# Reordering the set-up of a windowed-attention and feed-forward kernel on one Trainium2 core

## The chip, the core and the metric

The kernel runs on one core of one Trainium2 chip. A core has a matrix engine (TensorE, PE in the profile), a vector engine (VectorE, DVE), a scalar engine (ScalarE, ACT), a general engine (GpSimd, POOL) and a synchronising engine (SyncE, SP). Each runs its own list of instructions in order; they wait for one another and for transfers by semaphores. Transfers (DMA) are issued from POOL or SP in this kernel: the profile calls POOL's queue q0 and SP's q1. The metric is the device time of one execution in microseconds (us).

## The reference

There are 8 batches of 8 heads, 576 positions and head size 64, in float32. Position pairs count if they are at most 32 apart, or if one of the two is among 8 "global" positions given by index. A feed-forward layer with a sine follows.

```python
mask = np.abs(pos[:, None] - pos[None, :]) <= 32
mask = mask | is_global[:, None] | is_global[None, :]
scores = np.where(mask, scale * (q @ k.T), -1e9)
x = softmax(scores) @ v                     # then heads side by side: 4608 x 512
h = x @ w_in                                # 512 -> 2048
s = np.sin(alpha * h)
out = (h + s * s / (alpha + 1e-9)) @ w_out  # 2048 -> 512
```

## The kernel before

The order of the instructions is the order in which the program writes them down; no scheduler moves them. Work goes by batch. `attention(b)` computes the scores of a batch for four pairs of heads: 12 blocks of keys for a pair, in three groups of four (`scores`, a PSUM tile called `ring`). ACT takes the exponential (tile `E`), DVE multiplies by the 0/1 tile `MASK`, PE multiplies by V and sums (`products`, tiles `zn`, `zd`), ACT makes the reciprocal by Ln and Exp, and DVE writes the normalised result (`xT`, or `xlast` for odd batches). `gemm1(b)` is the first matrix product with the sine, in 16 steps (`nt`) of 128 columns. `gemm2(b)` is the second, and its matmuls are dealt out one by one between those of the next batch (`fill`).

For each batch the keys lie in a tile `KX`, the queries in `QX` and the values in `VX`, in two copies by parity of the batch. In each 64-wide block of `KX` and `VX` the last part holds the 8 global rows, so these have to be written there too. `KX` and `QX` of batch 0 come from natural loads (`nat`, in the tile `H2`, shown as `H`), which PE transposes (`turn_part`) and ACT and DVE copy into place (`place_part`). From batch 1 on, the keys and queries are cast in DRAM (`cast_qk`), transposed by DMA from SP's queue (`turn_qk`), and copied into place by DVE (`place`).

Three things concern the global rows. For batch 0, three indirect gathers by the row numbers in `grow` bring them as `g0k`, `g0q` and `VG0`; PE transposes the first two (tile `pg`) and ACT spreads them (`place_global_keys`, `place_global_queries`). For later batches, SP gathers the global rows of all batches (`gather` into `gk`, `gq`, `gv`), PE and DVE turn the first two into `kTg` and `qTg` (`turn_kq`), and POOL spreads them (`place_globals`). POOL casts `gv` to `VGb` (`cast_globals_v`), and `load_vg` copies rows of it into `VX` by SP's queue.

`MASK` is made in the set-up: six iotas on POOL (`qrel`, `qpos`, `jrow`), squares on ACT, and comparisons on DVE (`band`, and then a correction called `far`, for which the index lists `gp64` and `gidx8` have to be in). V, the four column blocks of `w_in` and the four row blocks of `w_out` are loaded from POOL's queue, each with a cast. A one-element copy `seen` on POOL waits for the transposed keys of batch 1; what POOL issues after it is held until then.

Of the kernel before, what the change touches and what calls it, by code (L numbers as in the profile page):

```python
# [10 lines left out]
ALU = mybir.AluOpType  # L11
AF = mybir.ActivationFunctionType
DT = mybir.dt
# [3 lines left out]
P = 128  # L17
KW = 96
NG = 8
KT = 48  # L20
WCOL = 120
# [4 lines left out]
PAD = 16  # L26
# [221 lines left out]
def kernel(  # L248
# [11 lines left out]
    nc = tc.nc  # L260
    B, H, S, D = q.shape
    DM, DFF = moe_w_in.shape
    WIN = 32
# [102 lines left out]
    def place_globals(b):  # L366

        for hp in range(NHP):
            for t in range(2):
                rows = slice(t * D, (t + 1) * D)  # L370
                nc.gpsimd.tensor_copy(
                    out=KX[b % 2][rows, hp, :, t * D + KT : t * D + KT + NG],
                    in_=kTg[rows, hp, None, :, b].to_broadcast([D, NT12, NG]),
                )
        for y in range(2):
            nc.gpsimd.tensor_copy(
                out=globals_of(b, slice(0, P), y),
                in_=qTg[:, :, None, y::2, b].to_broadcast([P, NHP, 7, 4]),
            )
# [67 lines left out]
    make_identity(nc, identb[:])  # L447
    qrel = setup.tile([P, 2, 2, WCOL // 2], DT.float32, name="qrel")
    for par, left in ((0, PAD), (1, 40)):
        nc.gpsimd.iota(qrel[:, par, :, 0:left], pattern=[[1, 2], [2, left]], base=-WIN,  # L450
                       channel_multiplier=0, allow_small_or_imprecise_dtypes=True)
        nc.gpsimd.iota(qrel[:, par, :, left:60], pattern=[[1, 2], [2, 60 - left]],
                       base=2 * left - 40, channel_multiplier=0, allow_small_or_imprecise_dtypes=True)
    qpos = setup.tile([P, NT12, 2, 24], DT.float32, name="qpos")
    nc.gpsimd.iota(qpos[:], pattern=[[KT, NT12], [1, 2], [2, 24]], base=0, channel_multiplier=0,
                   allow_small_or_imprecise_dtypes=True)
    jrow = setup.tile([P, NG], DT.float32, name="jrow")
    nc.gpsimd.iota(jrow[:], pattern=[[1, NG]], base=0, channel_multiplier=0,
                   allow_small_or_imprecise_dtypes=True)


    g64 = setup.tile([NG * B, 1], DT.int64, name="g64")
# [69 lines left out]
    )  # L532
    nc.vector.tensor_copy(out=grow[:], in_=rowf[0 : NG * B, 4:5])
    nc.vector.memset(kflat[:, half : 2 * half], 0.0)
    nc.vector.memset(tiny[:], TINY)
# [13 lines left out]

    g0 = {}  # L550
    for name, src in (("k", k), ("q", q), ("v", v)):
        g0[name] = VG0 if name == "v" else setup.tile([NG * B, D], DT.bfloat16, name="g0" + name)
        nc.gpsimd.indirect_dma_start(
            out=g0[name][:], out_offset=None, in_=src[0].rearrange("h s d -> (h s) d"),
            in_offset=bass.IndirectOffsetOnAxis(ap=grow[:, 0:1], axis=0),
        )
# [71 lines left out]
    def place_global_queries(t, copy):  # L628
        for y in range(2):
# [5 lines left out]
            )  # L635

    gpf = setup.tile([P, 1], DT.float32, name="gpf")
    nc.vector.tensor_copy(out=gpf[:], in_=gp64[:].bitcast(DT.int32)[:, 0:1])
    nc.scalar.activation(out=qpos[:], in_=qpos[:], func=AF.Square, bias=gpf[:, 0:1], scale=-1.0)
    gf = setup.tile([P, NG], DT.float32, name="gf")  # L640
    nc.vector.tensor_copy(out=gf[:], in_=gidx8[:].bitcast(DT.int32)[:, 0::2])
# [3 lines left out]
    )  # L645
    later = setup.tile([P, NG], DT.float32, name="later")
    nc.vector.tensor_scalar(
        out=later[:], in0=jrow[:], scalar1=pm, scalar2=float(-KT), op0=ALU.subtract, op1=ALU.is_ge
    )
# [3 lines left out]
    nc.vector.scalar_tensor_tensor(  # L653
        out=cond[:, 2:3], in0=pm, scalar=float(KT + NG - 1), in1=cond[:, 1:2], op0=ALU.is_le, op1=ALU.mult
    )
# [12 lines left out]
    turn_part(1, 0, views([zn[:, n, :] for n in range(2)]))  # L668
    for n in range(2):
        place_part(1, 0, n, act)  # L670
    turn_part(0, 0, views([zd[:, n, :] for n in range(2)]))
    for n in range(2):
        place_part(0, 0, n, dve)
    for w, name in ((1, "k"), (0, "q")):
        pg[w] = both[0:D, 32 + w * 64 : 64 + w * 64].bitcast(DT.bfloat16)
        nc.tensor.transpose(
            out=pg[w][:], in_=g0[name][:], identity=identb[0 : NG * B, 0 : NG * B]
        )
    nc.tensor.transpose(out=both[:, 0:NT], in_=arow[:], identity=idf[0:NT, 0:NT])
    for t in range(2):  # L680
        place_global_keys(t, act)
        place_global_queries(t, act)
    act(out=alphaT[:], in_=both[:, 0:NT])
    turn_part(0, 1, views([z[:] for z in zo]))
# [282 lines left out]
    def gemm1(b):  # L967
# [28 lines left out]
        for nt in range(NT):  # L996
# [217 lines left out]
```

## Time and profile before

| | us |
|---|---|
| median of three runs (lowest, highest) | 368.57 (367.44, 368.85) |
| the profiled execution | 368.04 |
| its span, first to last instruction | 366.3 |
| PE busy in the span | 337.0 (92%) |
| DVE, ACT, POOL busy | 283.8, 293.2, 138.2 |
| first key transpose on PE | 6.87 |
| first scores on PE | 16.14 |
| first step of `gemm1(0)` on PE | 33.30 |
| first scores of batch 1 on PE | 54.23 |

The span is shorter than the time of the execution by 1.74 us. A line of a timeline gives the start, the duration, the engine, the line of the program, the operation, what it writes and reads, and how many instructions were merged; in square brackets stands how long the engine sat idle before it, and what it waited for. A row of a DMA queue gives packets, megabytes and the time of the packets as a share of 16 DMA engines. The granted TensorE clock is 0.998 in this execution.

### The profile page before, as it was taken

To read this page: it belongs to the slowest core of one execution; us is meant where nothing else is said; L and a number is where in the kernel's file an instruction comes from. 1 tells how busy PE (TensorE), PEld (TensorE's weight loads), DVE (VectorE), ACT (ScalarE), POOL (GpSimd) and SP (SyncE) were. 2 spreads that over 40 slices of the span, in tenths; PEclk is the share of its full clock that TensorE was granted. 3 is DMA by queue.
4 is the path that set the end of the run, shared out by engine and by line. 5 is a ranking of instruction groups with operands and counts; after the bars stand their busy time and mean duration, and the time that the engine had idled before them with its cause. 6 is when DMAs were issued, how large, how long until landed. Compare 5 with 4: busy or idle time off the path is not lost.

```text
span 366.3 us, 8428 instructions
## 1 busy us (share of the span) xinstructions
PE 337.0 (92%) x3040; PEld 227.8 (62%) x3040; DVE 283.8 (77%) x621; ACT 293.2 (80%) x566; POOL 138.2 (38%) x246
## 2 busy tenths in 40 slices
PE   2578968999999899999999999999999999999993
PEld 2467655766567666767667756776676766655441
DVE  6776998598878877888887887888788866789560
ACT  7689997887888688887889887979888888879510
POOL 7983696568864532660076205720000000000001
PEclk9999999999999999999999999999999999999999
DMA  6999999999999794989198904638111001000311
GB/s 124 112 156 186 175 148 190 150 146 200 161 201 221 78 107 106 174 94 149 30 167 111 146 30 54 82 30 158 45 46 30 0 30 60 29 3 20 96 57 53
DMA packets 103579, 38.07 MB, mean 104 GB/s; under 512 B 94138, under 2 KB 98250, under 8 KB 103082
## 3 DMA queue, kind: packets, MB, share of 16 engines
q0 software_dynamic: 56640, 18.56, 44.1%
q1 hardware_dynamic: 46890, 18.89, 26.2%
q8 instruction: 26, 0.43, 0.5%
q14 instruction: 23, 0.19, 0.2%
HBM read 37.15 MB, written 17.83 MB: 150 GB/s over the span
## 4 chain that ended last, share of the span: by engine, by line
PE 66%; DVE 9%; ACT 5%; issue 2%; DMA 1%; POOL 0%; POOLq 0%; DVEq 0%; ACTq 0%
PE zo L1047 29%; PE zn L990 9%; PE zr L990 8%; PE zd L990 7%; PE zd L783 4%; PE ring L741 4%; PE zn L783 4%; DVE H L1028 3%; ACT sb L1020 2%; DVE QX L349 2%; DVE s L1026 1%; PE zr L783 1%; ACT osb L1053 1%; DVE xT L815 1%; ACT s L1024 1%
## 5 line engine op out<-in xcount | busy, mean ns | idle before, releaser
L1047 PE MATMUL zo<-w_out,H 128*128 128x512 bf16 x576 | 153.7, 379 | 0.0
L990 PEld LDWEIGHTS <-w_in 128*128 128x128 bf16 x1024 | 98.6, 98 | 47.1 <-issue 10.8
L393 POOL DMA_DIRECT2D VX<-in_v_dram x128 | 82.7, 657 | 90.8 <-PE zd L783 63.1
L1047 PEld LDWEIGHTS <-H 128*128 128x128 bf16 x576 | 52.3, 97 | 37.2
L749 ACT ACTIVATE E<-ring 128x480 bf16<-128x480 f32 x96 | 54.2, 567 | 23.0 <-PE ring L741 22.7
L752 DVE TENSOR_TENSOR E<-E,MASK 128x480 bf16<-128x480 bf16 x96 | 35.9, 405 | 17.5 <-ACT E L749 16.2
L1075 POOL DMA_INDIRECT out_dram<-osb,grow x1 | 1.0, 998 | 121.0 <-SPq L1182 121.0
L1028 DVE SCALAR_TENSOR_TENSOR H<-s,recipT,zn 128x576 bf16<-128x576 bf16 x47 | 38.2, 813 | 10.3 <-ACT s L1024 6.6
L1024 ACT ACTIVATE s<-sb 128x576 bf16<-128x576 bf16 (+1 forms) x62 | 42.7, 689 | 2.0
L741 PE MATMUL ring<-QX,KX 128*128 128x120 bf16 x384 | 37.2, 221 | 7.3 <-ACT E L749 3.2
L1020 ACT ACTIVATE sb<-zn,alphaT 128x576 bf16<-128x576 f32 (+1 forms) x47 | 34.8, 739 | 11.2 <-PE zn L990 11.2
L741 PEld LDWEIGHTS <-KX 128*128 128x128 bf16 x384 | 28.3, 100 | 23.0 <-issue 10.8
L1028 DVE SCALAR_TENSOR_TENSOR H<-s,recipT,zd 128x576 bf16<-128x576 bf16 x39 | 31.7, 814 | 6.5 <-ACT s L1024 4.6
L1028 DVE SCALAR_TENSOR_TENSOR H<-s,recipT,zr 128x576 bf16<-128x576 bf16 x39 | 31.7, 813 | 4.2 <-ACT s L1024 2.1
L1020 ACT ACTIVATE sb<-zd,alphaT 128x576 bf16<-128x576 f32 (+1 forms) x39 | 28.9, 740 | 7.1 <-PE zd L990 7.0
L1026 DVE TENSOR_TENSOR s<-sb 128x576 bf16<-128x576 bf16 (+1 forms) x66 | 30.6, 463 | 4.1 <-ACT sb L1020 3.8
L1020 ACT ACTIVATE sb<-zr,alphaT 128x576 bf16<-128x576 f32 (+1 forms) x39 | 28.9, 740 | 5.6 <-PE zr L990 5.6
L783 PEld LDWEIGHTS <-VX 128*128 128x128 bf16 x448 | 25.9, 98 | 9.3 <-issue 3.3
L990 PE MATMUL zn<-xT,w_in 128*128 128x288 bf16 x184 | 26.9, 286 | 3.5 <-DVE H L1028 2.0
L1053 ACT COPY osb<-zo 128x512 f32<-128x512 f32 x36 | 20.8, 577 | 11.3 <-PE zo L1047 10.0
L990 PE MATMUL zn<-xlast,w_in 128*128 128x288 bf16 (+1 forms) x192 | 28.8, 289 | 0.4
L783 PE MATMUL zn<-E,VX 128*128 128x120 bf16 (+2 forms) x336 | 26.3, 209 | 1.0 <-DMA VX<-VGb 0.6
(159 smaller groups left out, 489.9 us busy)
## 6 DMA issues: line engine op xcount, KB each, us to landing
VX<-in_v_dram POOLq DMA_DIRECT2D x128, 36.0 KB, 5.8
kd<-in_k_dram POOLq DMA_DIRECT2D x7, 576.0 KB, 7.3
qd<-in_q_dram POOLq DMA_DIRECT2D x7, 576.0 KB, 9.5
w_in<-in_moe_w_in_dram POOLq DMA_DIRECT2D x4, 512.0 KB, 5.7
w_out<-in_moe_w_out_dram POOLq DMA_DIRECT2D x4, 512.0 KB, 8.7
out_dram<-osb SPq DMA_DIRECT2D x8, 256.0 KB
out_dram<-osb SPq DMA_DIRECT2D x8, 224.0 KB
out_dram<-osb SPq DMA_DIRECT2D x8, 192.0 KB
```

Of the source, the lines that this page charges most:

```text
L393: nc.gpsimd.dma_start(out=VX[b % 2][r : r + 24, hp, :, t * D : t * D + D], in_=v[b, 2 * hp + t].rearrange("(i a y) d -> y a i d", a=24, y= ...
L741: nc.tensor.matmul(out=ps[:, e * WCOL : (e + 1) * WCOL], lhsT=kx[:, hp, i, :], rhs=qx[:, hp, :, s0 : s0 + 60], start=True, stop=True, skip ...
L749: nc.scalar.activation(out=Eg, in_=ps[:, 0 : 4 * WCOL], func=AF.Exp, scale=scale, accum_out=EA[:, n : n + 1])
L752: nc.vector.tensor_tensor(out=Eg, in0=Eg, in1=MASK[:, 4 * g : 4 * g + 4, :].rearrange("p i c -> p (i c)"), op=ALU.mult,)
L783: nc.tensor.matmul(out=out_t[:, half, :, a - half * CUT : z - half * CUT], lhsT=OB[:] if key else VXb[:, hp, i, :], rhs=E[:, i, :, a - s0 ...
L990: nc.tensor.matmul(out=h[e][:, 0:W], lhsT=lhsT, rhs=xT[:, c, e, 0:W], start=(c == 0), stop=(c == CT - 1), skip_group_check=True,)
L1020: nc.scalar.activation(out=sb[:, es, 0:W], in_=h[:, :, 0:W], func=AF.Sin, scale=alphaT[:, nt : nt + 1])
L1024: nc.scalar.activation(out=s2[:, :, 0:W], in_=sb[:, :, 0:W], func=AF.Square)
L1026: nc.vector.tensor_tensor(out=s2[:, :, 0:W], in0=sb[:, :, 0:W], in1=sb[:, :, 0:W], op=ALU.mult)
L1028: nc.vector.scalar_tensor_tensor(out=H2[:, nt, r0 : r0 + S].rearrange("p (e c) -> p e c", e=2)[:, es], in0=s2[:, es, 0:HALF], scalar=recip ...
L1047: nc.tensor.matmul(out=ops[:], lhsT=H2[:, nt, blk * P : (blk + 1) * P], rhs=w_out[:, nt, :], start=(nt == 0), stop=(nt == NT - 1),)
L1053: nc.scalar.copy(out=osb[:], in_=ops[:])
```

## The change

Instructions of the set-up and of the end of batch 0 are put in another order, and one group of copies is merged. The amount of computation is the same.

- On POOL the gathers of `g0k` and `g0q` stand right behind the computation of `grow`, and the six iotas behind them. The first block of `w_in` is issued next, then the gather of V's global rows, then V of pairs 0, 1 and 2.
- ACT clears the second half of `VX[0]` before it squares `qrel`.
- The key and query copies of batch 0 stand before the correction of `MASK`, which comes after the global columns. Two short comparisons and `gpf` stay ahead of the query copies.
- Block 2 of `w_in` is issued right behind the casts of batch 1, block 3 right behind POOL's memsets and before SP turns the keys and `seen` is written. Before, both came after `seen`. V of pair 1 of batch 1 moves from there to step 11 of `gemm1(0)`.
- At step 11 of `gemm1(0)`, the order on POOL was: four blocks of `w_out`, `cast_globals_v`, `place_globals(1)`. It becomes: block 0 of `w_out`, V of pair 1, `place_globals(1)`, `cast_globals_v`, blocks 1 to 3.
- `place_globals(1)` writes the keys of all four pairs with one copy for each half of the partitions: two copies of 64x384 in place of eight of 64x96.

```diff
     def place_globals(b):
-        for hp in range(NHP):
+        step = NHP if b == 1 else 1
+        for hp in range(0, NHP, step):
+            hps = slice(hp, hp + step)
             for t in range(2):
                 rows = slice(t * D, (t + 1) * D)
                 nc.gpsimd.tensor_copy(
-                    out=KX[b % 2][rows, hp, :, t * D + KT : t * D + KT + NG],
-                    in_=kTg[rows, hp, None, :, b].to_broadcast([D, NT12, NG]),
+                    out=KX[b % 2][rows, hps, :, t * D + KT : t * D + KT + NG],
+                    in_=kTg[rows, hps, None, :, b].to_broadcast([D, step, NT12, NG]),
                 )
...
-    def load_w_out():
-        for g in range(4):
+    def load_w_out(gs):
+        for g in gs:
...
     make_identity(nc, identb[:])
-    qrel = ...; qpos = ...; jrow = ...        # six iotas
...
     nc.vector.tensor_copy(out=grow[:], in_=rowf[0 : NG * B, 4:5])
+    g0 = {}
+    def gather_first(name, src):
+        g0[name] = VG0 if name == "v" else setup.tile([NG * B, D], DT.bfloat16, name="g0" + name)
+        nc.gpsimd.indirect_dma_start(...)
+    gather_first("k", k)
+    gather_first("q", q)
+    qrel = ...; qpos = ...; jrow = ...        # the same six iotas
...
-    g0 = {}
-    for name, src in (("k", k), ("q", q), ("v", v)):
-        ...indirect_dma_start(...)
+    load_w_in((0,))
+    gather_first("v", v)
+    clear(vflat[:, half : 2 * half])
     nc.scalar.activation(out=qrel[:], in_=qrel[:], func=AF.Square, bias=kpos[:, 0:1], scale=-1.0)
-    clear(vflat[:, half : 2 * half])
-    load_v(0, (0,))
-    load_w_in((0,))
-    load_v(0, (1, 2))
+    load_v(0, (0, 1, 2))
     load_w_in((1,))
     load_v(0, (3,))
     cast_qk(1)
+    load_w_in((2,))
     load_vg(0)
     gather(q, gq)
...
+    turn_part(1, 0, ...); place_part(1, 0, n, act)      # keys
+    later = ...; cond[:, 2:3] = ...
     gpf = ...
+    turn_part(0, 0, ...); place_part(0, 0, n, dve)      # queries
+    pg transposes, arow transpose
     nc.scalar.activation(out=qpos[:], in_=qpos[:], func=AF.Square, bias=gpf[:, 0:1], scale=-1.0)
+    place_global_keys, place_global_queries, alphaT     # ACT
     gf = ...; first = ...; fone = ...; far = ...; MASK = max(MASK, far)
-    later, cond: among these;  turn_part, place_part, pg, globals: behind these
     turn_part(0, 1, ...); turn_part(1, 1, ...)
...
             if b == 0 and nt == 11:
-                load_w_out()
+                load_w_out((0,))
+                load_v(1, (1,))
+                place_globals(1)
                 cast_globals_v()
-                place_globals(1)
+                load_w_out((1, 2, 3))
                 load_v(1, (2, 3))
                 load_vg(1)
...
                     nc.gpsimd.memset(KX[1][:].bitcast(DT.int32), 0)
+                    load_w_in((3,))
                     turn_qk(1)
                     nc.gpsimd.tensor_copy(out=seen[:], in_=turned[1][1][0:1, 0:1])
-                    load_w_in((2, 3))
-                    load_v(1, (0, 1))
+                    load_v(1, (0,))
                     gather(v, gv)
```

More of the change, by code (lines that the diff above doesn't have):

```diff
@@ L447 @@
     make_identity(nc, identb[:])
[L448 to L459, printed above, removed]
     g64 = setup.tile([NG * B, 1], DT.int64, name="g64")
@@ L533 @@
     nc.vector.tensor_copy(out=grow[:], in_=rowf[0 : NG * B, 4:5])
+    g0 = {}
+    def gather_first(name, src):
+        g0[name] = VG0 if name == "v" else setup.tile([NG * B, D], DT.bfloat16, name="g0" + name)
+        nc.gpsimd.indirect_dma_start(
+            out=g0[name][:], out_offset=None, in_=src[0].rearrange("h s d -> (h s) d"),
+            in_offset=bass.IndirectOffsetOnAxis(ap=grow[:, 0:1], axis=0),
+        )
+    gather_first("k", k)
+    gather_first("q", q)
+    qrel = setup.tile([P, 2, 2, WCOL // 2], DT.float32, name="qrel")
+    for par, left in ((0, PAD), (1, 40)):
+        nc.gpsimd.iota(qrel[:, par, :, 0:left], pattern=[[1, 2], [2, left]], base=-WIN,
+                       channel_multiplier=0, allow_small_or_imprecise_dtypes=True)
+        nc.gpsimd.iota(qrel[:, par, :, left:60], pattern=[[1, 2], [2, 60 - left]],
+                       base=2 * left - 40, channel_multiplier=0, allow_small_or_imprecise_dtypes=True)
+    qpos = setup.tile([P, NT12, 2, 24], DT.float32, name="qpos")
+    nc.gpsimd.iota(qpos[:], pattern=[[KT, NT12], [1, 2], [2, 24]], base=0, channel_multiplier=0,
+                   allow_small_or_imprecise_dtypes=True)
+    jrow = setup.tile([P, NG], DT.float32, name="jrow")
+    nc.gpsimd.iota(jrow[:], pattern=[[1, NG]], base=0, channel_multiplier=0,
+                   allow_small_or_imprecise_dtypes=True)
     nc.vector.memset(kflat[:, half : 2 * half], 0.0)
@@ L635, in place_global_queries @@
             )
+    turn_part(1, 0, views([zn[:, n, :] for n in range(2)]))
+    for n in range(2):
+        place_part(1, 0, n, act)
+    later = setup.tile([P, NG], DT.float32, name="later")
+    nc.vector.tensor_scalar(
+        out=later[:], in0=jrow[:], scalar1=pm, scalar2=float(-KT), op0=ALU.subtract, op1=ALU.is_ge
+    )
+    nc.vector.scalar_tensor_tensor(
+        out=cond[:, 2:3], in0=pm, scalar=float(KT + NG - 1), in1=cond[:, 1:2], op0=ALU.is_le, op1=ALU.mult
+    )
     gpf = setup.tile([P, 1], DT.float32, name="gpf")
     nc.vector.tensor_copy(out=gpf[:], in_=gp64[:].bitcast(DT.int32)[:, 0:1])
+    turn_part(0, 0, views([zd[:, n, :] for n in range(2)]))
+    for n in range(2):
+        place_part(0, 0, n, dve)
+    for w, name in ((1, "k"), (0, "q")):
+        pg[w] = both[0:D, 32 + w * 64 : 64 + w * 64].bitcast(DT.bfloat16)
+        nc.tensor.transpose(
+            out=pg[w][:], in_=g0[name][:], identity=identb[0 : NG * B, 0 : NG * B]
+        )
+    nc.tensor.transpose(out=both[:, 0:NT], in_=arow[:], identity=idf[0:NT, 0:NT])
     nc.scalar.activation(out=qpos[:], in_=qpos[:], func=AF.Square, bias=gpf[:, 0:1], scale=-1.0)
+    for t in range(2):
+        place_global_keys(t, act)
+        place_global_queries(t, act)
+    act(out=alphaT[:], in_=both[:, 0:NT])
     gf = setup.tile([P, NG], DT.float32, name="gf")
@@ L645 @@
     )
[L646 to L649, printed above, removed]
     nc.vector.tensor_tensor(out=first[:], in0=first[:], in1=later[:], op=ALU.max)
@@ L652 @@
     nc.vector.tensor_reduce(out=fone[:], in_=first[:], axis=AX.X, op=ALU.min)
-    nc.vector.scalar_tensor_tensor(
-        out=cond[:, 2:3], in0=pm, scalar=float(KT + NG - 1), in1=cond[:, 1:2], op0=ALU.is_le, op1=ALU.mult
-    )
     nc.vector.tensor_tensor(out=fone[:], in0=fone[:], in1=cond[:, 2:3], op=ALU.mult)
@@ L666 @@
         nc.vector.tensor_tensor(out=own, in0=own, in1=farv[:, :, e], op=ALU.max)
[L668 to L683, printed above, removed]
     turn_part(0, 1, views([z[:] for z in zo]))
```

5 lines of the change are left out of this document (removed).

## The prediction

> **What bounds the kernel now.** I read the page first, then the timeline of each engine over the first 100 us, then the waits, then the DMA queues in short windows.
>
> From the page, the span and TensorE's (PE's) busy tenths, one digit per 9.2 us:
>
> ```profile
> span 366.3 us, 8428 instructions
> PE   2578968999999899999999999999999999999993
> ```
>
> From the seventh slice on PE is full. The list of PE's waits after 62 us holds 3.3 us in all, 0.4 of it for the batch-1 step at 62.05. So whatever makes PE reach that step earlier moves the end by as much, and nothing later that the diff touches can help. The first 62 us are the place to look, and there the engines take turns. VectorE (DVE):
>
> ```profile
> 7.73 0.15 DVE L638 CAST gpf<-gp 128x1 f32<-128x1 int32 x1 [0.38 <-DMA gp<-in_global_idx_dram]
> 9.73 0.37 DVE L641 CAST gf<-gidx 128x8 f32<-128x8 int32 x1 [1.84 <-DMA gidx<-in_global_idx_dram]
> 12.26 3.73 DVE L611 COPY QX<-zd 64x288 bf16<-64x288 bf16 x8
> ```
>
> DVE waits 1.84 us for an index list, does mask steps until 12.26, and copies the queries only then. PE and ScalarE (ACT) over the same time:
>
> ```profile
> 11.73 0.26 PE L676 MATMUL pg<-identb,g0k 64*64 64x64 bf16 x1 [2.41 <-DMA g0k<-in_k_dram,grow]
> 13.26 1.13 PE L590 MATMUL zn<-identb,H 48*128 48x48 bf16 x24
> 16.14 0.95 PE L741 MATMUL ring<-QX,KX 128*128 128x120 bf16 x8 [1.75 <-DVE QX L611]
> 13.97 0.17 ACT L683 COPY alphaT<-pg 128x16 f32<-128x16 f32 x1
> 16.79 0.57 ACT L749 ACTIVATE E<-ring 128x480 bf16<-128x480 f32 x1 [2.65 <-PE ring L741]
> ```
>
> The first scores wait 1.75 us for DVE's query copies alone: PE is through its own transposes at 14.39, ACT with the global columns at 13.94. After 16.79 ACT is nearly gapless until the table load at 53.50 (0.86 us at 27.25, 0.33 us near 44). DVE is gapless from 46 to 56. So a shift of the first scores is carried through.
>
> Then the places at the other end of the stretch:
>
> ```profile
> 42.34 1.15 PE L990 MATMUL zn<-xT,w_in 128*128 128x288 bf16 x8 [0.74 <-DMA w_in<-in_moe_w_in_dram]
> 54.23 0.37 PE L741 MATMUL ring<-QX,KX 128*128 128x120 bf16 x4 [1.95 <-POOL QX L376]
> 57.78 0.36 PE L783 MATMUL zn<-E,VX 128*128 128x88 bf16 x4 [0.56 <-DMA VX<-VGb]
> 54.79 0.57 ACT L749 ACTIVATE E<-ring 128x480 bf16<-128x480 f32 x1
> 61.23 0.77 DVE xlast L815
> ```
>
> The 1.95 us wait for GpSimd (POOL) looks large but is free: ACT loads its table until 54.78 and takes the scores without a wait. The last line is from the chain of waits. Two chains meet there: DVE's copies and masks (gapless from 55.47), and PE's products at 57.78, then exp at 59.04, Ln, reciprocal until 61.1. The second has 0.1 us to spare.
>
> **The change, part by part.** Sums are against the profiled execution: 368.04 us, its span 366.3 and 1.74 around it. It lies 0.53 below the median of the three runs, 368.57.
>
> *Gathers ahead of the iotas.* They issue at 5.85, 7.13 and 8.43 now and take 5.8, 4.7 and 3.6 to land: 11.65, 11.83, 12.03. Issued 1.28 apart, they land 0.2 apart, just after the last of the four q and k loads in the same queue (issued 3.23, longest landing 8.3: 11.5). Issued from 4.4 (identity done 4.33, `grow` 4.07) they land behind the same load: worth 0. If landing followed the issue, the pg transposes would come 1.4 earlier and query copies and ACT's globals would bound at about 13.75: at most 0.6 more.
>
> *Iotas behind two gathers.* Two issues of 1.28 from 4.4 reach 6.7 (with 0.97 for the second); four iotas, 0.6: qrel at 7.3 instead of 4.9. ACT meanwhile does the clear that was put ahead (4.9 to 6.4); its Square of 0.49 ends at 7.85. DVE: band to MASK 1.1 (6.25 to 7.35 now), three small ops 0.5, so query copies run from 9.5, 3.73 long, to 13.3. POOL's issue beside a DVE memset could be slower; the nearest row, q and k loads issued beside L528's memset, shows none (0.52 against 0.55 elsewhere); if each gather waited out the memset at 4.34 to 5.68, all this slips 1.3 and 0.45 of the gain goes.
>
> *Key copies and qpos on ACT.* Keys 8.0 to 11.2, the qpos Square then 0.78 to 12.0: hidden by the g0k wait; the global copies start at 12.40 as now.
>
> So QX is ready at 13.3, the globals at 13.94, and PE's transposes end last, at 14.39: scores **1.75 earlier**. The mask steps come after: 13.3 plus 2.1 (the 2.53 from 9.73 to 12.26 less two ops moved out) plus 0.45 of recipT: 15.9, against the first exp done at 15.7. The 0.15 is made up by the third tile, which waits for ACT.
>
> *First w_in block ahead of V.* Issued at about 8.3 instead of 12.0, same bytes. V for pair 0 then lands near 17.5 against a demand of 21.2; v's gather lands near 16.3, and SP reaches its copies at 15.88 in any case (k gather 8.87 to 15.76). Worth 0.
>
> *w_in 2 and 3 ahead of the turned keys.* Today both issue at 36.62, after `seen` (36.38). Issued near 24 and 31, block 2 lands before 39.6, where PE would now want it; the 0.74 wait goes. ACT had 0.33 idle behind it, DVE 0.15: **0.2**. What pays: the key and query turning on SP's queue (5,081 packets in 31 to 38.2, with 22 of the other queue's beside them) now shares the engines with 1 MB. Turned batch-2 tensors, issued beside loads, took 5.34 and 5.56 to issue instead of 3.31 and 2.50, so I expect up to 5 us of delay. kt, in by 36.4 now, would be in by 41.4, and DVE wants it at 44.8: hidden. The v gather that SP issues next is not safe (rival B). POOL's memsets of the batch-1 buffers (24.0 to 30.5) start 0.8 later for block 2; POOL then waits for `seen` anyway.
>
> *Globals on POOL.* Eight copies of 0.39 become two of 64x384: between 0.47 (ACT's copy of that shape) and 4 x 0.39 = 1.56 each; I take 1.1, scaling the elements over a 0.15 fixed part (the jrow iota). They start when DVE has cast kTg and qTg, 1.95 earlier than 49.9 to 50.2, and end at 50.9 where ACT's table load would cover up to about 52.3. Worth 0. V of pair 1 (four issues of 0.65) and w_out 0 go ahead, in a time when POOL waited on landings.
>
> *The cast of VGb now follows place_globals*: done at 51.5, against 50.37. SP's copies of VGb wait for it, and PE for the first two of these. Now they are issued from 50.40 and land at 57.78. This is the one disputed cost:
>
> ```profile
> q0 software_dynamic: 780, 0.77, 111.8%
> ...
> q0 software_dynamic: 794, 0.80, 118.5%
> q1 hardware_dynamic: 382, 0.05, 15.2%
> ```
>
> The first line is 50.4 to 54.8, the others 55 to 59 (packets, MB, share). SP's queue, q1, moved nothing for 4.5 us while four w_out loads filled q0, then about 95 packets a us beside it, 96 to a copy. In the change the first copy is issued with w_out 1 only being issued (0.77 each), so its packets should go first, as the batch-0 copies did (issue 15.88, packets from 16.6): both landed by about 54.9, with 55.8 (57.78 less 1.95) as the point of no loss. The Trainium skill (DMA: Bandwidth & Descriptors, section Queues, rings and completion order) says each DMA engine alternates between queues packet by packet. By that rule the wait of 4.5 us should not be there; the trace shows it for the start of a transfer and agrees with the rule afterwards. By the rule the copies land in time and the sum stays; by the row, rival C.
>
> *w_out 1 to 3 behind the globals.* Four took 46.7 to 60.9, some 3 us each; three from 52.4 land near 56, 59 and 62. PE would want them at 59.2, 62.4 and 63.5, V of pair 2 at 64.3 behind them. Hidden, by 1.5 at the tightest.
>
> Sum: 1.75 + 0.2 = 1.95 us. The profiled execution goes to 366.1, the median to **366.6**.
>
> **The rivals.** *A, more is gained (13%, 365.5).* The gathers land early (0.6), or PE gets fast earlier: its four-tile score groups take 0.56 until 24 us and 0.37 from 26.84, and the 0.86 of ACT idle at 27.25 comes from the slow part. I take the switch at 4.2 us after the restart at 22.60, as the rows have it, moving with the work, and 0.5 to either side. The Trainium skill (TensorE: Matmul & The Clock Gate, Part 1) puts the switch at the end of a free-running window of about 3.4 us; by it the switch need not move with the work, and no single trace can say.
>
> *B, half is given back (18%, 367.6).* The turning, crowded by w_in, delays the v gather: SP's qt ends at up to 41.5 instead of 36.5, and eight gathers that landed by 48.4 land near 51.5 to 52. POOL, in order, then holds the cast, the copies of VGb and w_out 1 to 3 about 1 us: 1.95 - 1.0. For it: q1 moves nothing from 14 to 16, while w_in 0 is under way. Against it: the gather was in 1.3 before the cast at 49.74. That the gathers of the change don't bring the global rows any earlier is no rival, it is in the sum.
>
> *C, slower than before (26%, 370.5).* The copies of VGb stand behind w_out for 7.4 us again, as from 50.40 to 57.78: issued at 51.5, landed at 58.9, 3.1 after the point of no loss, on the chain with 0.1 to spare. Alone that is 3.1 - 1.95 = 1.2 slower (369.7); with B's late gather ahead of it (52.8 to 60.2) it is 2.5 slower (371.1); 370.5 is between. It decides as soon as w_out 1's descriptors reach the engines before the first copy's. For it: the 4.5 us without a packet. Against it: then four loads stood in the queue, now none.
>
> **How the numbers follow.** The forecast has 43%. A half per cent, 1.84 us, is what a measurement of this kernel can tell from no change; 366.73 is that line, and the forecast lies on it: two thirds of it and A make 0.42 faster. C with the late gather, two thirds of C, makes 0.17 slower. The rest of both and B are 0.41. Range: from A's gains together (1.95 + 0.6 + 0.5) with 0.3 for the spread of the runs, 365.2, to C's middle, 370.5, which leaves out 0.13 above and some 0.04 below. The forecast's own range is 366.0 to 367.3.
>
> **What would show it.** Right: first scores at 14.4 with no wait for DVE; g0k still near 11.6; no w_in wait near 40; place_globals in two copies of about 1.1; VGb copies landed before 55.8; the step at 62.05 now at 60.1. Wrong: scores bound by qrel or ACT; the cast waiting for v's gather; PE waiting 2 us or more for VX<-VGb or w_out; a slow PE for longer than 4.2 us.

## Result and the profile after

| | before | changed |
|---|---|---|
| median, same chip (us) | 368.28 | 371.59 |
| lowest to highest | 367.44 to 368.85 | 371.07 to 379.8 |
| profiled execution, its span | 368.04, 366.3 | 371.73, 370.0 |

The ratio is 1.0086, 95% interval 1.0061 to 1.011: the change makes the kernel 3.2 us slower. Two of the six executions of the changed kernel, at 376.9 and 379.8, are in the median of the table but left out of the ratio.

The page of the changed kernel (span, and PE's busy share in 40 slices) shows the loss in one place: the seventh digit, some 55 to 65 us, is 4 where before had 8.

```profile
span 370.0 us, 8379 instructions
PE   2678964999999899999999999999999999999993
```

The head did what it was moved for. From the timelines of PE and DVE (start, duration, engine, line, operation, and in brackets the idle time before it):

```profile
12.30 0.26 PE L660 MATMUL pg<-identb,g0k 64*64 64x64 bf16 x1 [2.77 <-DMA g0k<-in_k_dram,grow]
14.90 0.98 PE L745 MATMUL ring<-QX,KX 128*128 128x120 bf16 x8
9.75 3.73 DVE L617 COPY QX<-zd 64x288 bf16<-64x288 bf16 x8 [0.23 <-PE zd L596]
```

The first scores start at 14.90 (16.14 before), with no wait for DVE. PE's groups (several matmuls that the timeline merges) become fast at 24.4 (26.8 before), the first step of `gemm1(0)` comes at 31.52 (33.30), the wait of 0.74 for `w_in` is gone, and the first exp of batch 1 stands at 52.88 (54.79). Up to there 1.8 to 1.9 us are won.

Then SP's queue and POOL, from their timelines. The kernel before first:

```profile
30.57 3.31 SPq L339 DMA_TRANSPOSE kt<-kd  x1
33.98 2.50 SPq L339 DMA_TRANSPOSE qt<-qd  x1
...
36.38 0.18 POOL L1118 COPY seen<-kt 1x1 bf16<-1x1 bf16 x1 [5.89 <-DMA kt<-kd]
...
49.74 0.63 POOL L695 CAST VGb<-H 64x512 bf16<-64x512 f32 x1
```

and the changed kernel:

```profile
32.12 6.54 SPq L339 DMA_TRANSPOSE kt<-kd  x1
38.76 2.24 SPq L339 DMA_TRANSPOSE qt<-qd  x1
41.19 7.09 SPq L476 DMA_DIRECT2D H<-in_v_dram  x8
...
52.85 14.64 SPq L404 DMA_DIRECT2D VX<-VGb  x16
```

```profile
40.94 0.18 POOL L1125 COPY seen<-kt 1x1 bf16<-1x1 bf16 x1 [10.35 <-DMA kt<-kd]
47.58 1.76 POOL L373 COPY KX<-kTg 64x384 bf16<-64x384 bf16 x2
52.21 0.61 POOL L699 CAST VGb<-H 64x512 bf16<-64x512 f32 x1 [2.04 <-DMA H<-in_v_dram]
52.77 2.28 POOL L418 DMA_DIRECT2D w_out<-in_moe_w_out_dram  x3
```

The turning of the keys takes 6.54 us to issue (3.31 before), `seen` comes at 40.94 (36.38 before), and the gather of V's global rows starts 4.5 later. Not all of that is the slower turning: it also starts at 32.12 instead of 30.57, after SP has waited 3.1 us for the gather of the query rows to land. The cast of `VGb` waits 2.04 us for V's gather. Before, the cast waited for nothing and was done at 50.37. The copies of `VGb` follow at 52.85 (50.40), and three blocks of `w_out` are issued in the same moment. The chain of waits runs through exactly these pieces (start, duration, what):

```profile
47.61 4.54 DMA H<-in_v_dram
52.21 0.62 POOL VGb L699
52.85 0.67 SPq L404
53.56 6.46 DMA VX<-VGb
```

6.46 us for a copy of 12 KB. The queues in windows of 1 us (packets, MB, time of the packets as a share of 16 engines), here 56 to 57 and 57 to 58, show it waiting beside `w_out`:

```profile
q0 software_dynamic: 171, 0.18, 115.3%
q1 hardware_dynamic: 16, 0.00, 2.4%
...
q0 software_dynamic: 197, 0.19, 119.5%
q1 hardware_dynamic: 6, 0.00, 1.0%
```

A copy has 96 packets. From 54 to 60 q1 moved 16, 72, 16, 6, 48 and 96 in each microsecond: 88 packets by 56, 22 more by 58, and the 192 of two copies only after 59, when one block of `w_out` had landed (POOL, which waits for it, goes on at 59.12). PE's timeline shows what that costs:

```profile
54.92 0.38 PE L557 MATMUL zo<-ones 128*128 128x512 bf16 x1
60.16 0.53 PE L787 MATMUL zn<-E,VX 128*128 128x88 bf16 x4 [4.86 <-DMA VX<-VGb]
...
61.66 0.60 PE L745 MATMUL ring<-QX,KX 128*128 128x120 bf16 x4
...
65.86 0.36 PE L787 MATMUL zn<-E,VX 128*128 128x88 bf16 x4
```

PE waits 4.86 us (0.56 before) and starts the first products of batch 1 at 60.16 instead of 57.78. Then it is slow: a group of four score tiles takes 0.60 instead of 0.37, and the granted clock from 60 to 66 is 0.56 (the third number from the right; in shorter windows it is 0.50 from 58.5 to 65.3 and 1.00 on either side):

```profile
60.00:66.00 6.00, 5.62 (x48) 4.40 (x50) 1.71 (x5) 3.16 (x9) 1.68 (x3) 0.56 1.49 163
```

The next step, at 62.05 before, comes at 65.86. From first products to that step it is 5.70 us against 4.27, so of the 3.81 that are lost, 2.38 are there when the copies arrive, and 1.43 come behind them, where PE is slow. After that everything runs as before; the span is 3.7 longer.

### The profile page after: what moved, and what is told of

Its sections match the earlier page's. It is cut to its first block, busy times and chain, and to the rows that moved or that the text cites. A ratio compares the mean times of both kernels' runs of the same rounds, so it can differ in the third digit from the quotient of the medians.

```text
span 370.0 us, 8379 instructions
## 1 busy us (share of the span) xinstructions
PE 336.2 (91%) x2995; PEld 229.2 (62%) x3040; DVE 284.7 (77%) x621; ACT 293.8 (79%) x566; POOL 137.6 (37%) x240
## 4 chain that ended last, share of the span: by engine, by line
PE 60%; DMA 11%; DVE 9%; ACT 7%; SPq 6%; issue 5%; POOL 1%; POOLq 0%; DVEq 0%; ACTq 0%
PE zo L1053 26%; PE zn L994 9%; PE zr L994 6%; PE zd L994 6%; PE ring L745 4%; PE zd L787 4%; DVE H L1034 4%; DMA out_dram<-osb 4%; PE zn L787 3%; DMA H<-in_q_dram 3%; ACT sb L1026 3%; SPq L339 3%; DMA g0k<-in_k_dram,grow 2%; DMA VX<-VGb 2%; SPq L476 2%
## 5 line engine op out<-in xcount | busy, mean ns | idle before, releaser
L1053 PE MATMUL zo<-w_out,H 128*128 128x512 bf16 x531 | 143.9, 379 | 1.9
L787 PEld LDWEIGHTS <-VX 128*128 128x128 bf16 x448 | 26.4, 99 | 13.3 <-issue 7.4
## 6 DMA issues: line engine op xcount, KB each, us to landing
qd<-in_q_dram POOLq DMA_DIRECT2D x7, 576.0 KB, 10.8
```

Source lines behind the costliest of these rows:

```text
L787: nc.tensor.matmul(out=out_t[:, half, :, a - half * CUT : z - half * CUT], lhsT=OB[:] if key else VXb[:, hp, i, :], rhs=E[:, i, :, a - s0 ...
L1053: nc.tensor.matmul(out=ops[:], lhsT=H2[:, nt, blk * P : (blk + 1) * P], rhs=w_out[:, nt, :], start=(nt == 0), stop=(nt == NT - 1),)
```

## The experiments

The theory after the first look had three parts. **Block 3 beside the turning**: transfers of `w_in` that run beside the turning of keys and queries make both crawl, so the gather, the cast and what POOL issues behind it come late. **Copies beside w_out**: the copies of `VGb` take some 7 us whenever `w_out` moves beside them, however early they are issued. **Head given back**: without a better tail the 1.8 us of the head end in a wait for the globals. The rivals were that the late gather alone delays the copies, that block 2 or the casts are to blame, and that holding `w_out` and V behind the globals costs time by itself. Ratios are against the kernel before, whose median in each comparison lay between 367.64 and 368.39; in brackets the 95% interval.

### Both blocks of w_in back behind `seen`

```diff
-                    load_w_in((3,))
                     turn_qk(1)
                     seen
+                    load_w_in((2, 3))
```
(and block 2 no longer behind `cast_qk(1)`)

> The changed kernel with blocks 2 and 3 of w_in back behind the one-element copy that waits for the turned keys. Theory 1 (two delays in series: the blocks of w_in hold up SP's turning and with it V's gather, 3.6 us; and the copies of VGb, started together with blocks 1 to 3 of w_out, take about 7 us to land instead of 2.5): the cast no longer waits for the gather and ends near 50.8 instead of 52.8, but the copies still land 7 us after their issue, near 58, so PE waits about 3 us for them; time 368 to 370. Rival 2 (only the late gather costs, the copies were late because of it): copies land by 54, no wait, 366.6. Rival 3 (w_out behind the globals is what costs): PE waits on w_out and the time stays at 371.

Measured: 370.12, ratio 1.0047 [1.0019, 1.0076]. `seen` is back at 35.38 and the gather is in time. But block 2 is late for the earlier PE (a wait of 2.01 at 42.46), `kTg` comes late for POOL (2.92), and the cast ends at 52.7 for that reason. The copies are issued at 52.74, with no gather in their way, and PE gets them at 59.71 after a wait of 1.68: 7.0 us from issue to use. So the copies are slow by themselves, the late gather only adds to it.

### The kernel before with blocks 2 and 3 ahead of the turning

```diff
+    load_w_in((2,))                 # behind cast_qk(1)
...
+                    load_w_in((3,))
                     turn_qk(1)
                     seen
-                    load_w_in((2, 3))
```

> The kernel before with nothing but the blocks 2 and 3 of w_in moved ahead of the turning. Theory 1: the wait of 0.74 us for w_in goes, but V's gather lands near 52 instead of 48.5, the cast (which here stands ahead of the globals of keys and queries) waits for it and ends near 52.8, the globals end near 56.6 instead of 54.2, the copies of VGb land near 59 to 60: slower, 370 to 371. Rival 2b (the crowding was made by the shifted head, not by w_in): same as before or 0.2 faster, 368.1.

Measured: 379.91, ratio 1.0311 [1.023, 1.0392]. The direction is as expected, the size is missed by 9 us. SP's and POOL's timelines:

```profile
29.19 6.87 SPq L339 DMA_TRANSPOSE kt<-kd  x1
36.17 12.03 SPq L339 DMA_TRANSPOSE qt<-qd  x1
...
48.15 0.18 POOL L1120 COPY seen<-kt 1x1 bf16<-1x1 bf16 x1 [16.94 <-DMA kt<-kd]
```

and its queues from 36 to 38:

```profile
q1 hardware_dynamic: 247, 0.06, 78.6%
q0 software_dynamic: 113, 0.12, 42.9%
```

In the kernel before, q1 moved 1,957 packets from 34 to 36 at 120.6%. That is 1.206 x 32 us / 1,957 = 20 ns of engine time for a packet; here it is 0.786 x 32 / 247 = 102 ns. Both queues crawl for ten microseconds. `seen` comes 11.8 us later, and as four blocks of `w_out` and the globals follow it in POOL's order, PE waits 10.4 us for `QX` at 64.77. This is the change's edit with its cover taken away. In the changed kernel, with the same edit, `seen` came 4.6 us later than before, 1.55 of that by the later start of the turning.

### The kernel before with the new head alone

```diff
+    key and query copies, gathers, iotas, globals in the new order (up to the first scores)
     block 2 and 3 of w_in, and tile 11 of gemm1(0): as before
```

> The kernel before with the new order of the first 16 us alone (gathers, iotas, first block of w_in, query copies, mask steps); all that follows on POOL and SP as before. Theory 1 with POOL's list as the pin: the first scores come 1.2 earlier and gemm1(0) ends 1.8 earlier, but the globals still end at 54.2 and the copies of VGb land at 57.8, as what POOL does after 24 us doesn't move; so at the batch-1 step almost all of it is given back: gain 0 to 0.5, 367.8 to 368.3. Rival 4 (as the prediction had it, a shift of the head is carried through): 366.5.

Measured: 368.14 against 368.28, ratio 0.9994 [0.9965, 1.0023]: as expected, the gain is given back.

```profile
42.38 1.15 PE L993 MATMUL zn<-xT,w_in 128*128 128x288 bf16 x8 [1.99 <-DMA w_in<-in_moe_w_in_dram]
...
54.45 0.37 PE L744 MATMUL ring<-QX,KX 128*128 128x120 bf16 x4 [2.71 <-POOL QX L378]
```

The first step of `gemm1(0)` is at 32.10, but the scores of batch 1 stand at 54.45, where they were (54.23). The wait for POOL's globals, 1.95 before and free beside ACT's table load, takes 0.76 more. So the edits at the tail are needed; the question is which.

### Gather of V's global rows ahead of the turning, cast and copies early

```diff
+                    gather(v, gv)
                     turn_qk(1)
                     seen
                     load_v(1, (0,))
+                    cast_globals_v()
+                    load_vg(1)
-                    gather(v, gv)
```
(the cast and the copies no longer at step 11)

> The changed kernel, with V's gather put ahead of the turning on SP, and the cast to VGb and the eight copies of it put behind V of pair 0, so well ahead of blocks 1 to 3 of w_out. Theory 1: the gather lands near 40, the copies near 50, before PE wants them at 55.3; the 4.9 us wait goes, PE stays fast, and the whole shift of the head remains: 366 to 366.6, faster than both kernels. Rival 3 (w_out 1 to 3 behind the globals costs by itself): a wait on w_out of 1 to 3 us appears in the place of the other, 367.5 to 370. Rival 5 (the turning, now behind the gather, is late for DVE's key copies at 44.7): DVE waits there, 367 to 369.

Measured: 371.18, ratio 1.007 [1.0037, 1.0103]: a miss. The copies were issued at 48.72, with one block of `w_out` (issued at 48.63) beside them instead of three; q1 had moved 130 packets by 54 and 335 by 55, and PE, which was late itself, never waited for them. But the gather, put ahead of the turning, took from 29.00 to 38.7, and the turning came behind it: `seen` at 44.79.

```profile
54.65 0.37 PE L745 MATMUL ring<-QX,KX 128*128 128x120 bf16 x4 [3.61 <-POOL QX L378]
67.38 1.02 PE L1051 MATMUL zo<-w_out,H 128*128 128x512 bf16 x4 [1.13 <-DMA w_out<-in_moe_w_out_dram]
69.52 0.36 PE L787 MATMUL zn<-E,VX 128*128 128x88 bf16 x4 [1.11 <-DMA VX<-in_v_dram]
```

One wait was removed and three others took its place, all by what POOL issued later.

### Blocks 1 to 3 of w_out behind V of pairs 2 and 3

```diff
                 cast_globals_v()
-                load_w_out((1, 2, 3))
                 load_v(1, (2, 3))
                 load_vg(1)
+                load_w_out((1, 2, 3))
```

> The changed kernel with blocks 1 to 3 of w_out behind V of pairs 2 and 3, so that nothing of w_out is issued beside the first copies of VGb. Theory 1b (copies that start together with w_out's blocks wait for them): issued near 52.9 as before, the first two now land within 3.5 us, by 56.4, and PE's wait for them falls from 4.9 us to 1.5 or less; in its place PE waits for w_out, whose block 1 is issued near 58 and lands near 64: time 370 to 373. Rival 6 (the copies take 7 us whatever is beside them): PE's wait stays near 4.9.

Measured: 373.31 (371.74 to 383.04), ratio 1.0152 [1.0131, 1.0174], at the upper end of the expected 370 to 373. The profiled execution is the one at 383.04, with 381.3 us of span; the other four end at 373.71. So it says nothing on the copies. It says something else: this kernel's order is that of the changed kernel up to 44 us, and here `seen` came at 50.38 instead of 40.94, with 9.67 and 10.78 us for the two turnings. So the same order can collide more in one execution than in another; how often it goes that far isn't known from one profile.

### Only block 3 back behind `seen`

```diff
-                    load_w_in((3,))
                     turn_qk(1)
                     seen
+                    load_w_in((3,))
                     load_v(1, (0,))
```

> The changed kernel with block 3 of w_in alone back behind the one-element copy; block 2 stays ahead. Theory 7 (the turning crawls only while a block of w_in moves beside it, and block 3 is the one that overlaps): the turned keys are in by 38 instead of 40.9, V's gather by 49 instead of 52, the cast no longer waits and ends near 50.8; the copies still start with w_out and land near 57.8, PE waits about 2.8: 369 to 370. Rival 8 (block 2 holds it): keys in at 40 or later, time 371 to 372.

Measured: 369.09, ratio 1.0038 [1.0023, 1.0053], span 367.7: in the expected 369 to 370. From SP's, POOL's and PE's timelines:

```profile
32.22 3.50 SPq L339 DMA_TRANSPOSE kt<-kd  x1
...
50.27 0.61 POOL L699 CAST VGb<-H 64x512 bf16<-64x512 f32 x1
...
57.95 0.36 PE L787 MATMUL zn<-E,VX 128*128 128x88 bf16 x4 [2.35 <-DMA VX<-VGb]
```

The turning takes 3.50 again, though it still starts late (32.22), and the cast waits for nothing. What is left is the second part, with its slow PE (groups of 0.60 and a granted clock of 0.50 from 59.0 to 62.4; the step of 62.05 is at 62.90): the copies are issued at 50.90 and used at 57.95, 7.05 us later. That is the same 7 us as in the changed kernel (52.85 to 60.16) and with both blocks back (52.74 to 59.71), whatever stood ahead of it.

### The kernel before with block 3 alone ahead of the turning

```diff
+                    load_w_in((3,))
                     turn_qk(1)
                     seen
-                    load_w_in((2, 3))
+                    load_w_in((2,))
```

> The kernel before with block 3 of w_in alone moved ahead of the turning (block 2 behind, as before). Theory 7: half a megabyte beside the turning instead of a whole one, all of it overlapping: the turned keys come 4 to 6 us later than 36.4 and the time is 372 to 375, about half of what both blocks cost. Rival 8: keys within 1 us of 36.4, but block 2 late as before, 368 to 369.

Measured, in two executions: 374.02, ratio 1.017 [1.0117, 1.0222]: in the expected range. `seen` comes at 42.41, 6.0 later, and block 2 behind it is late:

```profile
33.68 8.86 SPq L339 DMA_TRANSPOSE qt<-qd  x1
...
48.62 2.10 PE L990 MATMUL zn<-xT,w_in 128*128 128x288 bf16 x8 [8.41 <-DMA w_in<-in_moe_w_in_dram]
```

One block of 512 KB is enough for the crawl. The total is not the price of the crawl alone, since block 2 was also put behind it.

### A reordering of all of it

```diff
+    load_w_in((2,))                       # ahead of cast_qk(1)
...
+                    gather(v, gv)
                     turn_qk(1)
                     seen
+                    load_w_in((3,));  load_v(1, (0,));  cast_globals_v();  load_vg(1)
...
+                load_w_out((0, 1));  place_globals(1);  load_w_out((2,));  load_v(1, (1,))
+                load_w_out((3,));  load_v(1, (2, 3))
```

> The changed kernel with the transfers kept apart: block 2 of w_in ahead of the casts of batch 1 (so that it has moved before the turning starts), V's gather ahead of the turning, block 3, V of pair 0, the cast and the copies of VGb behind the one-element copy, then blocks 0 and 1 of w_out, the globals, block 2, V of pair 1, block 3, V of the rest. If theories 1 and 7 hold, no transfer moves beside the turning, the copies land near 48, w_out is ahead of PE, and the shift of the head stays: 366 to 366.6, faster than both kernels. If w_out or V comes late in its place: 367 to 369, with the wait on PE to show for it.

Measured: 373.45, ratio 1.0157 [1.0136, 1.0178]: a miss. The gather ahead of the turning took 10.84 us (29.17 to 40.0), `seen` came at 45.87, and block 3 behind it made PE wait 6.15 us at 51.79. In all runs that keep the gather behind the turning, the same eight transfers were issued within 6.8 to 7.4. The difference is a wait: 4.2 of the 10.84 us SP stood, by the profile, until the gather of the query rows had landed (2.7 of 9.69 in the run before with the gather ahead); the rest, 6.6 and 7.0, is what the gather takes anywhere, and here the turning stands behind it. Keeping transfers apart by holding them back has a price too.

### Cast ahead of the globals

```diff
                 load_w_out((0,));  load_v(1, (1,))
+                cast_globals_v()
                 place_globals(1)
-                cast_globals_v()
                 load_w_out((1, 2, 3))
```
(on top of block 3 behind `seen`)

> The changed kernel with two edits: block 3 of w_in behind the one-element copy (as in the run with block 3 back), and the cast to VGb, and with it the start of its copies, ahead of the globals of keys and queries, so about 2.5 us ahead of w_out's block 1. Theory 1b: the cast ends near 49.5, the first two copies land by 53.5 with nothing of w_out beside them, before PE wants them at 55.5; PE's wait of 2.4 us goes, the globals end near 52.5 in ACT's shadow, and the head's gain stays: 366.3 to 367, faster than both kernels. Rival 3 (w_out behind the globals costs by itself): PE waits on w_out instead and it stays near 369.

Measured: 371.91, ratio 1.0086 [1.0065, 1.0108]: a miss. The copies, issued at 50.63 with no `w_out` beside them until 53, moved 31, 177 and 123 packets in the three microseconds from 51 on, and PE did not wait for them: the second part holds. But POOL stood 3.96 us for the gather before the cast, with the globals behind it:

```profile
53.15 0.56 PE L745 MATMUL ring<-QX,KX 128*128 128x120 bf16 x4 [3.30 <-POOL QX L378]
...
68.57 0.36 PE L787 MATMUL zn<-E,VX 128*128 128x88 bf16 x4 [1.63 <-DMA VX<-in_v_dram]
```

PE, after 3.30 us idle, was slow until 58.7, and `w_out` and V, issued from 53.05, came late for it (0.20 and 1.63). Between 51 and 54 POOL's queue had carried nothing: the rival that holding them back costs by itself is true as well.

### The kernel before with this tail alone

```diff
     head: as before
+    tile 11 of gemm1(0), blocks of w_in, place_globals(1): as in the run above
```

> The kernel before with its own first 16 us, and the transfers and the POOL order after that as in the run with the cast first. If head and tail need each other: the globals and copies come earlier, but exp and DVE are as late as before, so only the wait for w_in goes: 0 to 0.5 faster than before, 367.3 to 368. If the tail brings gain by itself: 366.5.

Measured: 372.23, ratio 1.0097 [1.008, 1.0114]: a miss again, by the same waits (3.93 for `QX`, 1.62 for `w_out`, 1.54 for V). With the head as before, `seen` came at 40.29, and the turning of the keys took 6.44 to issue: block 2, still behind the casts, was moving beside it (164 and 176 packets a microsecond on POOL's queue from 32 to 34).

### Blocks 1 to 3 of w_out last, with block 3 of w_in behind `seen`

```diff
                 place_globals(1);  cast_globals_v()
-                load_w_out((1, 2, 3))
                 load_v(1, (2, 3));  load_vg(1)
+                load_w_out((1, 2, 3))
```

> The run with block 3 back, but with blocks 1 to 3 of w_out issued only behind V of pairs 2 and 3. Theory 1b: the first two copies of VGb, issued at 50.9 as there, land by 54.5 instead of 57.9, and PE doesn't wait for them; it waits for w_out later, 2 to 5 us, time 370 to 373. Rival 6 (they take 7 us whatever stands beside them): PE's wait of 2.4 us for them stays.

Measured: 371.58, ratio 1.0078 [1.006, 1.0096]. Issued at 52.06, 1.2 later than with block 3 alone moved back, the copies cost PE nothing: with V beside them in place of `w_out` q1 moved 104 and 141 packets in the microseconds from 53 on, so both were in before 55. `w_out` is then late three times, 5.0 us in all in the profiled execution (the longest of four, at 373.87), the longest of them here:

```profile
70.35 1.16 PE L1053 MATMUL zo<-w_out,H 128*128 128x512 bf16 x4 [2.62 <-DMA w_out<-in_moe_w_out_dram]
```

### One block of w_out early, two late

The last order takes each part at its word. Block 3 of `w_in` stays behind `seen`, one block of `w_out` fills the stretch in which POOL's queue was empty, and only V is issued beside the first copies.

```diff
                 load_w_out((0,));  load_v(1, (1,))
+                load_w_out((1,))
                 place_globals(1);  cast_globals_v()
-                load_w_out((1, 2, 3))
-                load_v(1, (2, 3));  load_vg(1)
+                load_v(1, (2,));  load_w_out((2, 3));  load_v(1, (3,));  load_vg(1)
```

> The changed kernel with block 3 of w_in behind `seen` (as in the run that came out at 367.7 us of span) and GpSimdE's order at tile 11: w_out 0, V pair 1, w_out 1, globals, cast, V pair 2, w_out 2 and 3, V pair 3. Theory (block 3 late to the turning; copies slowed only by w_out traffic beside them; w_out and V in time if the empty stretch of GpSimdE's queue from 48 to 52 us is filled by w_out 1): the cast at about 50.5 to 51 without a wait for the gather, the copies behind the light traffic of V pair 2 landing within 5 us (by 56.5), at most 0.5 us of PE's wait for them at the first batch-1 step, no w_out wait over 0.5 us, and 366.5 to 367.5 us, 0.5 to 1.5 below the kernel before. Rival (any POOL transfer started beside the copies holds them as long as three blocks do): the wait of 2 us or more at the first batch-1 step is back, 369 or more. Rival (w_out 1 beside the gather of the globals' values delays the cast as block 3 of w_in did): the cast waits for the gather until 52 or later, 369 to 371.

Measured: 367.17 against 368.1, ratio 0.9977 [0.9962, 0.9993]; span 364.1, 365.79 for the profiled execution, the shortest of twelve. The gain is small, but the interval lies below 1: it beats both kernels. POOL's and PE's timelines:

```profile
47.27 0.78 POOL L418 DMA_DIRECT2D w_out<-in_moe_w_out_dram  x1 [0.16 <-DVE kTg L711]
...
50.51 0.61 POOL L699 CAST VGb<-H 64x512 bf16<-64x512 f32 x1
51.07 2.69 POOL L395 DMA_DIRECT2D VX<-in_v_dram  x4
53.74 1.56 POOL L418 DMA_DIRECT2D w_out<-in_moe_w_out_dram  x2
...
55.24 0.36 PE L787 MATMUL zn<-E,VX 128*128 128x88 bf16 x4
...
60.26 0.36 PE L787 MATMUL zn<-E,VX 128*128 128x88 bf16 x4 [0.33 <-DVE xlast L819]
```

and its queues from 52 to 53 and from 53 to 54:

```profile
q0 software_dynamic: 328, 0.12, 92.4%
q1 hardware_dynamic: 36, 0.00, 5.8%
...
q0 software_dynamic: 582, 0.07, 97.9%
q1 hardware_dynamic: 157, 0.02, 25.2%
```

36 and 157 make 193 packets: both copies are in at 54, 2.9 us after the issue at 51.14. PE has no wait for them, none for `w_out` and none for POOL. The step that stood at 62.05 is at 60.26. Neither rival of this run appeared.

In ratios of the timed runs, three kernels, each one step from the one before, give the sum of the change: with block 3 back the loss falls from 0.86% to 0.38%, 1.8 us; with `w_out` spread around the copies from 0.38% to -0.23%, 2.2 us; what is left is a gain of 0.9 us. The three were timed in separate comparisons, each against the kernel before.

## Why the prediction was wrong

**Head: right in its sum, by two errors that happen to cancel.** The query copies were put at 9.5 to 13.3 (9.75 to 13.48 measured), `qrel`'s Square at 7.3 (7.32). The gathers were put at no gain, since they land behind the k and q loads: issued 1.35 us earlier, `g0k` was used at 12.30 instead of 11.73, so 0.6 later; why isn't shown. PE's transposes behind it then ended late, and the first scores came 1.24 earlier, not 1.75. In return PE became fast 2.4 earlier, the second half of rival A. The restart of the scores, from which the prediction counted the 4.2 us to the switch, came only 1.2 earlier (21.40 instead of 22.60), so the switch did not just move with the work, as the forecast took it. That it is the clock isn't shown: the granted clock reads 1.00 there in both traces, and only the lengths of the groups tell. With that 1.78 was there at the first step of `gemm1(0)`. Of the 0.2 for `w_in`, 0.13 was there: 1.91 at the first exp of batch 1. The last order shows the sum as it was meant: the step predicted for 60.1 came at 60.26, and a span of 366.3 - 1.95 = 364.35 was 364.1. Only half of that is in its median: 0.23% of 368.1 is 0.85 us. The profiled execution is the best of twelve, and what the others lose wasn't seen.

**Globals: right.** Two copies of 0.88 (predicted 1.1), no wait of PE for them in the changed kernel.

**The failed step: "its packets should go first, as the batch-0 copies did".** The first copy of `VGb` did begin at 54, beside 55 packets of `w_out`, and 88 packets had moved by 56. Forecast were both copies, 192 packets, by 54.9. From 56 to 58 only 22 more moved. An early start isn't enough. With three blocks of `w_out` beside the copies three runs gave 7.0 to 7.3 us from issue to use. With one block beside them (gather ahead of the turning) the 192 packets took 5.3 to 6.3 us. With none issued beside them (cast first, `w_out` last, and the spread order) they took under 3. The Trainium skill (DMA: Bandwidth & Descriptors, section Queues, rings and completion order) has each DMA engine alternate between queues packet by packet. In the trace the shares were 22 against 368 packets from 56 to 58, and 144 against 340 from 58 to 60: equal turns, as the prediction read the rule, did not come, also once the transfer had started, where the prediction still took the trace to agree. That page's packet is a run of descriptors; how many of the profile's packets it holds isn't shown, so the rule itself stays open.

**The failed cover: up to 5 us of turning "hidden", the gather "not safe".** The crowding was seen, and `seen` 4.6 later lies within its "up to 5", though 1.55 of it is the later start of the turning, which no term had; the turning itself took 3.0 more. It was given to rival B, 18%, at a price of 1.0, and combined with C at 17%. It was the ordinary case: with block 3 ahead of the turning `seen` was late in the changed kernel and in the three others that leave the gather behind it, by 4.6 to 11.8, and by 14 in the execution at 383.04. The row that told of it was in the prediction (turned tensors beside loads took 5.34 and 5.56 to issue instead of 3.31 and 2.50); it should have been followed to POOL's cast as the likely case.

**Rival C with the late gather is what happened, and its price was too small.** It had the copies from 52.8 to 60.2; they were issued at 52.85 and used at 60.16. It put the step 2.5 later, at 64.5; it came at 65.86. The missing 1.4 is a term that no case had: PE, idle for 4.86 us, ran slow afterwards, 1.43 by the two lengths above. The Trainium skill (TensorE: Matmul & The Clock Gate, Part 1) has PE's clock halve after a free-running window of about 3.4 us that is idle. The granted clock agrees: it falls to 0.50 at 58.5, in the wait, 3.2 us after PE fell idle at 55.3. The traces show the slow stretch after shorter waits as well (2.35 with block 3 back, 2.71 with the head alone, there from 1.0 and 1.4 us after the wait had ended), where no stretch of 3.4 us was idle; there the measurement decides. The last order has a wait of 2.20 at 51.74 and no slow stretch behind it.

**Blocks 1 to 3 of `w_out` "hidden by 1.5".** In the changed kernel nobody waited for them, since PE was late itself. In two other orders, where they were issued from 53.05 (cast first) and 57.10 (`w_out` last), V was late by 1.6 and `w_out` by 5.0. So the cover was thin, as stated.

## What to carry over

Moving a load to an earlier place in a queue is costed by what runs beside it there, and by everything that the delayed transfer then holds in order: here 512 KB beside a DMA transposition delayed a gather, the gather a cast, and the cast three loads and a copy of 12 KB. Where a small copy is needed soon, look at which transfers will be moving while it moves, not only at which was issued first, and give the large ones a stretch in which the queue is empty. If PE will idle for some two microseconds or more, allow for a slow stretch behind the wait: here it cost 1.4 us more than the wait itself.

## What the runs showed of the hardware

- A DMA transposition and a casting load beside it slow each other: 20 ns of engine time for a transposing packet alone, 102 ns beside `w_in`, and 247 and 113 packets (0.18 MB) in 2 us on the two queues where the transposition alone had 1,957 (0.49 MB).
- How far it goes can differ between executions of the same order: `seen` at 40.94 in one and at 50.38 in another, unusually long one.
- The copies of `VGb` (96 packets each) moved 6 to 96 packets a microsecond beside three blocks of `w_out` (1 KB a packet), 104 to 171 beside V (some 120 bytes a packet; 157 in the last order), and up to 177 alone.
- PE's granted clock fell to 0.50 for some 3.4 us (55.9 to 59.3 with the head alone, 59.0 to 62.4 with block 3 back) or some 6.8 us (58.5 to 65.3 in the changed kernel, 51.9 to 58.7 with the cast first), beginning within the wait or up to 1.4 us after its end. The length of the wait alone does not decide: waits of 1.63 us (cast first, at 68.57) and 1.70 us (blocks 2 and 3 ahead of the turning in the kernel before, at 48.19) were followed by such a stretch, waits of 2.01 (both blocks back, at 42.46) and 2.20 (last order) were not.
- Eight small gathers in a row were issued within 6.8 to 7.4 us behind the turning. Ahead of it they took 9.7 and 10.8, of which 2.7 and 4.2 were a wait for an earlier gather to land.
